# Attention and a phase mixer on one core: shared DMA time in the plan, V by halves, casts on VectorE, fewer fillers

## The chip, the cores and the metric

The kernel runs on one core of a Trainium2 chip. The metric is the time that the device needs for one execution, in microseconds (us). The unprofiled times of one kernel scatter by up to some per cent, and each comes with the mean clock that TensorE (called PE in the profile) was granted. A run is called slow when it is over 1.5% above the fastest of the same kernel.

## The reference

Four batches of 768 positions, eight heads of 64. Heads 0, 2 and 6 attend to everything before them; heads 1, 3, 4, 5 and 7 only to four sink positions and a window of 64. The attention's result goes, head beside head, into a mixer:

```python
scores = np.where(mask, scale * q @ k.T, -1e9)          # mask: causal, or causal & (sink | window)
a = np.exp(scores - max); a = a / (a.sum(-1) + 1e-9)
x = (a @ v)                                             # heads side by side: 768 x 512 per batch
theta = x @ w_theta
zr, zi = x * np.cos(theta), x * np.sin(theta)
u = x + w_tok_r @ zr + w_tok_i @ zi                     # 768 x 768 mixing over positions
out = u + np.maximum(u @ w_ch, 0.0)
```

## The kernel before

The program is a list of more than 800 steps. Each step names the engines that can do it with an estimated duration, what it comes after, and which buffer it takes and gives back. A planner simulates the engines and, whenever one is free, gives it the ready step of highest rank. The resulting order is what the chip runs, engine by engine, and every engine runs its own list strictly in order. The rank is the length of the chain behind a step plus a correction from `TILT`, a list of numbers that an earlier search had found for exactly these durations. Transfers are steps too: "DMA" stands for the queue that GpSimd fills, "DMAH" for the one that SyncE fills.

```python
class Plan:
    COLD = 6000
    SHARE = {}                                   # empty: the branch below never runs
    ...
    def order(self, free):
        ...
                ns = s.on[e]
                if e == "PE" and t < self.COLD:
                    ns *= 1.9
                if e in self.SHARE:              # what the other kind of queue has to do slows this one
                    o = "DMA" if e == "DMAH" else "DMAH"
                    rest = max(0, free.get(o, 0) - t) + sum(...)
                    ns += min(rest, ns * self.SHARE[e]) * (1 - 1 / self.SHARE[e])
```

V of batches 1 to 3 arrives as float32 in one load, is cast to bf16 in four steps of one head pair each (pairs 0+2, 4+6, 1+3, 5+7), and for the five windowed heads a copy `vx` shifted by 64 rows is then made by DMA (the "V move").

```python
        issue = add("SP", 1000, lambda b=b: load_v(b), free_room)
        land = add("DMAH", 8500, None, [issue])
        for n in range(4):
            cast[b, n] = add({"DVE": 480, "POOL": 800}, 0, lambda b=b, n=n: cast_v(b, n), [land] + old, port=True)
        move = add("SP", 1400, lambda b=b: move_v(b), [cast[b, n] for n in (1, 2, 3)] + old)
        moved = add("DMAH", 700, None, [move])
```

Each 128 rows of x go through a transposing DMA into `xT`, for which the plan allowed `add("DMAH", 500, ...)`. Last, where the plan leaves PE idle in the first 30 us, small products without use ("fillers") keep its clock up:

```python
                gap = s.start - busy
                for _ in range(int(gap / 56 * (1 if s.start < 6000 else 0.55))):
                    nc.tensor.matmul(state["idle"][:, :128], ident, ident, start=True, stop=True, skip_group_check=True)
```

The softmax here doesn't subtract the row's maximum and nothing guards it: scores larger than these inputs give would overflow.

Of the kernel before, what the change touches and what calls it, by code (L numbers as in the profile page):

```python
# [25 lines left out]
    -1302, 9909, -1288, -485, 13881, -764, -420, 9549, 13866, 13674, -766, 9551, -9999629, -11630, 0, -913,  # L26
    -11392, 0, -838, 16670, 0, 18999, 0, 31553, -118, 18390, 640, 18361, 17120, 323, 17600, -382, 481, -706, 443,
    -106, 9627, 814, 9657, 561, 2712, 11002, 1146, 772, 492, 1364, 10980, 2378, 11128, 1607, 13772, 5395, 13972,
    5537, 14415, 116734, 16250, 190868, 16177, 80777, 16221, 81513, 392888, 392964, 393917, 393918, 393999, -9479,
    13017, 1168, 12237, 1256, 392649, 10167, 15325, 358, 154648, 429569, -944, 317644, 109627, 1628, 121764, 304,  # L30
    6684, 1805, -213, 0, -243, 0, 48, 0, 268, 2243, 82, 2385, -458, 8, 474, 3988, 15, -215, -298, 0, 1141, 0,
    1856, 0, 1833, 0, 2261, 0, 150, -110, 34, 1686, 2273, 0, 156, -506, -27, -122, -1317, 0, 29087, -609, 0, 4040,
    1057, 1017, 11085, 892, 1518, 554, 1866, -646, 10484, 973, -161, 1791, 1115, -348, 614, 9710, 273623, 9763,
    273460, 14943, 268995, 1069, 1272, 1670, -621, 917, -1392, 1300, 983, 828, 1721, 1204, 788, 13914, 116160,
    13800, 116248, 319905, 111468, 410534, 92438, 428932, 109116, 206113, 142, 317187, 5760, 95832, 2897, 206133,
    7063, 206110, 1716, 206004, -201, 578, 725, 95792, -153, 4546, 243, 95843, 4630, 12925, 22009, 3179, 4454,
    3981, 4172, 4669, 3945, 12929, 301, 3855, 860, 4395, 8714, 2367, 321, 336, 968, 531, 1019, 706, 1009, 206458,
    2077, 206456, 473, 45, 812, 62, 8, -736, 51, 1089, 27, 1778, 891, -55, 1165, -48, 893, -175, -527, 1, 930,
    488, 1010, -62, -733, 382, -249, 0, -685, 717, 1710, -588, 901, 678, 114, 765, 1226, -416, 2106, 938, 1642,
    -315, 1648, 377, -426, 8555, 6819, 2225, 611, 25, 2373, 610, 2258, 523, 709, 1335, 1069, 937, 1050, -298, 532,  # L40
    698, -479, 1572, 983, -715, 2138, 1252, -496, 2446, 4894, -495, 8639, -356, -672, 0, 1234, 5787, -413, 0, 410,
    1675, 1271, 414, 48, 388, 1109, 0, 1477, 626, 1756, 0, 1663, -672, 1819, 0, 1293, 1448, 465, 475, 1243, 1837,
    1295, 162, 1889, 467, 1488, 4474, -383, 1510, -898, 1679, 1682, 1256, 573, 1163, 106, 991, 1250, 445, 1896,
    1055, -143, 2305, 0, 1729, 0, 1172, -41, 1235, 673, -1178, 70, 0, 62, 1728, 885, -356, 621, -59, 12, -872,
    366, -367, 160, -781, -729, 0, 1888, 1965, 931, 1361, 796, 350, 0, 461, -397, 1765, 147, -912, -1367, 0, 947,
    370, 406, 0, 32, 2165, 1039, 535, -222, 4588, 7, 1380, -1639, 0, 91, 161, -49, 1198, -4, -922, 1691, 649, 704,
    0, 598, 1002, 656, 1201, 287, 259, 1980, 537, 695, 0, 162, -2, 160, 398, 403, 869, 183, -829, 396, 278, -834,
    230, 5365, -163, 208, -483, 1861, -530, -483, -2386, 61, -372, -292, -419, -428, -1803, 2, 102, 83, 2198, 431,
    -499, 196, 3468, 868, 259, 772, -1907, 445, -604, 103, 476, -183, 1596, -419, -629, 473, -1976, 9, 2203, 1423,
    984, -133, -560, -699, 147, -398, 97, 532, -1951, -128, 2407, -470, -605, 985, 34, 30, 208, -902, 353, 1767,  # L50
    961, 503, 0, 926, 644, 286, 0, 971, 686, -365, 168, 2865, 887, -284, 3557, 2492, 781, -517, 13, 2255, 1030,
    581, 0, 1052, 2526, 4485, 16764, 1082, 3775, 824, 1247, 11161, 15066, 16794, 18329, 1257, 1430, 1589, 1445,
    3273, 962, 3878, 3597, -465, 3254, -275, 1070, 789, 1102, 1172, 495, 253, 2635, 1324, -549, -338, 100, -173,
    46, 916, 0, 566, 177, -474, 961, 476, -674, 0, 192, 166, 0, -257, 1298, 1455, 0, 536, 273, -666, 568, 0, -951,
    0, -115, -237, 0, 885, 1254, 1597, 0, 226, -184, 1211, 1032, 0, 353, 8, 536, 25, 5, 606, 1260, 940, 0, -318,
    -1004, -993, -1256, 524, 1632, 2091, 553, 306, 0, 1218, 3158, 3117, 646, -614, 2310, 2208, -678, 60, 0, -178,
    3288, 1765, -435, 1010, -528, -134, 2674, 1241, -142, 1700, 650, 1333, 430, 612, 4107, 608, 1342, -164, 922,
    0, 1402, 1418, -709, 1482, 1386, 226, 7011, 123, 2034, 2021, 237, 643, 2159, 1363, 1292, 6888, 3610, -364,
    1026, 2201, 257, 1596, 2209, 925, -719, -151, 2611, 870, 6865, 104, 2247, 3477, 1105, -118, 756, -437, 2154,
    2252, 1513, 168, 7028, 109, 1623, 929, -291, 164, -139, -42, -664, 2046, -672, -57, 208, 793, 807, -552, 76,  # L60
    1555, 979, -786, 149, 1012, 864, 783, 0, 2261, 681, 1275, 6, 2544, 965, -732, 238, 767, -899, 148, 163, 1194,
    307, 1350, 1346, 1481, 1334, 323, 442, 732, 100, 145, 2068, 427, 1946, 3128, 3466, 2104, 2543, 2274, 2477,
    6630, 6388, 2865, -1355, -823, 1522, 1309, -646, 206, 0, 2095, 1904, 665, 23, -1439, 166, -303, 421, -695, 0,
    2218, 2187, 2190, -354, -462, 781, 877, -163, 58, 0, 1127, 692, 2301, 317, -800, 1688, 727, 1856, 880, 0, 38,
    898, 4483, 3686, 135, 4057, 1486, 1226, -116, 0, 796, 661, -2275, -343, -404, 2023, -2016, 404, 1710, 0, 1321,
    1355, 2252, 1553, -616, 1656, 2292, 819, 1306, 0, -680, 359, 1262, 1443, -321, 108, 1175, 589, 1409, 0, -1239,
    -1201, -978, 424, 138, 902, 1222, 138, 891, 0, 2070, 1612, 1785, 865, 480, 983, 4723, 835, 1272, 590, 2316,
    2562, 3059, 885, 4524, 478, 896, 652, 1003, 340, 845, 3709, 3073, 510, -99, 3191, 518, 961, 1059, 492,
# [3 lines left out]
class Step:  # L72
# [6 lines left out]
    def __init__(self, on, fn, after, take, give, mode, bias, port):  # L79
        self.on, self.fn, self.after = on, fn, [a for a in after if a is not None]  # L80
        self.take, self.give, self.mode, self.bias, self.port = take, list(give), mode, bias, port
        self.eng = next(iter(on)) if len(on) == 1 else None
        self.users = 0
        self.slot = self.start = self.end = self.ns = None


class Plan:
# [12 lines left out]
    SHARE = {}  # L100
# [6 lines left out]
    def add(self, on, ns, fn, after=(), take=None, give=(), mode=None, bias=0, port=False):  # L107
        s = Step(on if isinstance(on, dict) else {on: ns}, fn, after, take, give, mode, bias, port)
        for g in s.give:
            g.users += 1  # L110
        self.steps.append(s)
        return s

    def order(self, free):
# [18 lines left out]
        mode = {}  # L133
# [9 lines left out]
        out = []  # L143
# [7 lines left out]
        while events:  # L151
# [10 lines left out]
            for e in engines:  # L162
# [34 lines left out]
                if e in self.SHARE:  # L197
                    o = "DMA" if e == "DMAH" else "DMAH"
                    rest = max(0, free.get(o, 0) - t) + sum(n.on[o] for n in ready.get(o, ()) if ready_at[n.n].get(o, 0) <= t)
                    ns += min(rest, ns * self.SHARE[e]) * (1 - 1 / self.SHARE[e])  # L200
# [26 lines left out]
def kernel(  # L227
# [127 lines left out]
    def load_v(b):  # L355
        nc.sync.dma_start(out=v_room.rearrange("p h j d -> p (h j) d"), in_=v[b].rearrange("h (j p) d -> p (h j) d", p=128))
# [10 lines left out]
    def move_v(b):  # L367
        for s, h in ((slice(0, 1), slice(4, 5)), (slice(1, 5), slice(1, 8, 2))):
            nc.sync.dma_start(out=vx[:64, s], in_=vt[:64, h])
            nc.sync.dma_start(out=vx[64:, s, 1:], in_=vt[64:, h, :NB - 1])  # L370
# [340 lines left out]
    clear_vs_done = add({"DVE": 700, "POOL": 1900}, 0, clear_vs)  # L711
# [11 lines left out]
    for what in "kq":  # L723
        issue = add("SP", 600, lambda what=what: load_first(what), take="st_v", bias=10 ** 6)
        land = add("DMAH", 640, None, [issue])
# [12 lines left out]
    def cast_load(ns, moved, fn, take=None):  # L738
        issue = add("POOL", ns, fn, casting[-1:], take=take, bias=10 ** 6 if len(casting) < 8 else 0)
        casting.append(issue)  # L740
        return issue, add("DMA", moved, None, [issue])
# [30 lines left out]
    def v_steps(b):  # L772
# [9 lines left out]
        free_room = [cast[b - 1, n] for n in range(4)] + [xk[b - 1, 5]] if b > 1 else picked + room  # L782
        issue = add("SP", 1000, lambda b=b: load_v(b), free_room)
        land = add("DMAH", 8500, None, [issue])
        for n in range(4):
            cast[b, n] = add({"DVE": 480, "POOL": 800}, 0, lambda b=b, n=n: cast_v(b, n), [land] + old, port=True)
# [194 lines left out]
```

## Time and profile before

| | before |
|---|---|
| times of four runs, us | 201.62, 202.88, 200.8, 201.1 |
| profiled run: span, mean PE clock | 201.2 us, 0.983 |
| PE busy | 187.3 us (93%) |
| VectorE busy | 130.8 us (65%) |
| DMA | 28.07 MB in 42,302 packets |
| fillers | 106, of them 58 before the first transposes |

How to read it: PE is the engine that can hardly be shortened, so the 14 us in which it was not busy, and the microseconds in which it was busy at half speed, are what there is to win. The prediction shows the lines and prices three holes in PE's row: A at 60 to 68 us, B at 116 to 123 us and C at 91 to 93 us. The profiled run took 203.02 us and is on record as slow. Its low clock stands directly behind holes A and B.

### The profile page before, as it was taken

What the parts mean: (1) busy time and instruction counts of PE and PEld (TensorE: products, weight loads), DVE (VectorE), ACT (ScalarE), POOL (GpSimd) and SP (SyncE); (2) the same over time, 40 slices, a digit from 0 to 9 for tenths busy, and PEclk for the clock granted to TensorE, in tenths of its full rate; (3) what the DMA queues carried; (4) which work ended last, traced back from release to release, by engine and by line L of the source; (5) the groups of instructions that cost most, each with busy time, mean ns of one, the idle gap of its engine ahead of it and who ended that gap; (6) DMA issues with size and microseconds to landing.
All of it is one profiled execution on the core that took longest, in us unless ns stands there. A gap on an engine that the chain in (4) does not pass through costs nothing.

```text
span 201.2 us, 5192 instructions
## 1 busy us (share of the span) xinstructions
PE 187.3 (93%) x2177; PEld 106.8 (53%) x2177; DVE 130.8 (65%) x246; ACT 105.9 (53%) x130; POOL 61.9 (31%) x136
## 2 busy tenths in 40 slices
PE   7999999899995999996999939999999999999982
PEld 7866687545553884442436714554445564444440
DVE  6655597698783775988725720999535748962451
ACT  4597956798772369794555105696573444400010
POOL 7787879031595020163069000023121100000000
PEclk9999999999999799999999988999999999999999
DMA  5999999999389754953259993598453462324422
GB/s 166 156 176 189 205 207 165 162 236 232 63 136 204 96 81 137 224 156 73 104 73 141 158 187 77 146 220 152 101 154 89 114 91 79 103 80 111 127 104 104
DMA packets 42302, 28.07 MB, mean 139 GB/s; under 512 B 21928, under 2 KB 39208, under 8 KB 42280
## 3 DMA queue, kind: packets, MB, share of 16 engines
q1 hardware_dynamic: 29384, 17.65, 38.1%
q0 software_dynamic: 12896, 10.09, 35.0%
q8 instruction: 17, 0.28, 0.6%
q14 instruction: 5, 0.04, 0.1%
HBM read 25.71 MB, written 6.29 MB: 159 GB/s over the span
## 4 chain that ended last, share of the span: by engine, by line
PE 80%; DMA 8%; DVE 7%; ACT 2%; issue 1%; SPq 0%; POOL 0%; DVEq 0%
PE bank L595 27%; PE pair L572 10%; PE bank L618 10%; PE pair L455 9%; PE pair L546 7%; PE bank L388 7%; DMA xT<-x 5%; PE bank L939 4%; DMA vx<-vt 3%; DVE zr L319 2%; PE bank L342 2%; DVE zi L319 2%; DVE vx L316 1%; PE bank L608 1%; PE bank L639 1%; PE bank L558 1%
## 5 line engine op out<-in xcount | busy, mean ns | idle before, releaser
L595 PE MATMUL bank<-zr,wtokTr 128*128 128x512 bf16 x144 | 38.7, 380 | 1.5 <-DVE zr L319 1.5
L595 PE MATMUL bank<-zi,wtokTi 128*128 128x512 bf16 x144 | 38.8, 382 | 0.0
L323 POOL TENSOR_SCALAR_AFFINE_SELECT P<-P 128x256 bf16<-128x256 bf16 (+1 forms) x48 | 17.4, 383 | 49.0 <-ACT P L477 37.2
L477 ACT ACTIVATE P<-pair 128x1024 bf16<-128x1024 f32 (+2 forms) x24 | 21.4, 917 | 14.5 <-PE pair L455 14.5
L572 PE MATMUL pair<-w_theta_sb,xT 128*128 128x512 bf16 x96 | 24.0, 396 | 3.4 <-DMA xT<-x 3.4
L599 DVE TENSOR_TENSOR u<-x,bank 128x512 bf16<-128x512 bf16 x24 | 16.3, 684 | 14.5 <-PE bank L595 14.4
L618 PE MATMUL bank<-w_ch_sb,uT 128*128 128x512 bf16 x96 | 24.5, 380 | 0.7 <-ACT uT L316 0.7
L455 PE MATMUL pair<-qT,kT 64*64 64x128 bf16 (+6 forms) x380 | 24.4, 239 | 0.0
L319 DVE TENSOR_TENSOR zr<-x,ct 128x512 bf16<-128x512 bf16 x24 | 17.1, 745 | 9.8 <-ACT ct L577 9.8
L595 PEld LDWEIGHTS <-wtokTi 128*128 128x128 bf16 x144 | 13.4, 98 | 16.1 <-issue 0.7
L595 PEld LDWEIGHTS <-wtokTr 128*128 128x128 bf16 x144 | 12.9, 98 | 16.6 <-issue 3.2
L622 DVE SCALAR_TENSOR_TENSOR ot<-bank,u 128x512 f32<-128x512 f32 x24 | 16.5, 689 | 5.8 <-PE bank L618 5.4
L577 ACT ACTIVATE ct<-pair,half_pi 128x1024 f32<-128x1024 f32 x12 | 13.3, 1114 | 12.6 <-PE pair L572 10.3
L455 PEld LDWEIGHTS <-kT 64*64 64x64 bf16 (+1 forms) x380 | 12.2, 102 | 14.0 <-issue 10.1
L546 PE MATMUL pair<-vx,P_st 128*128 128x65 bf16 x120 | 15.3, 195 | 2.0 <-DMA vx<-vt 2.0
L553 DVE TENSOR_TENSOR x<-pair,r 128x512 bf16<-128x512 f32 x24 | 16.6, 692 | 0.8
L572 PEld LDWEIGHTS <-xT 128*128 128x128 bf16 x96 | 9.3, 101 | 14.7 <-DMA xT<-x 3.5
L377 POOL COPY kS<-kT 64x4 bf16<-64x4 bf16 x20 | 4.9, 247 | 39.4 <-DVE kT L316 27.7
L319 DVE TENSOR_TENSOR zi<-x,st 128x512 bf16<-128x512 bf16 x24 | 16.9, 735 | 0.0
L474 ACT ACTIVATE P_st<-pair 128x512 bf16<-128x512 f32 (+1 forms) x16 | 12.6, 810 | 6.0 <-PE pair L455 5.9
L546 PE MATMUL pair<-vt,P_st 128*128 128x65 bf16 x120 | 15.4, 195 | 0.0
L546 PE MATMUL pair<-vt,P 128*128 128x65 bf16 x252 | 14.3, 195 | 0.0
(90 smaller groups left out, 296.0 us busy)
## 6 DMA issues: line engine op xcount, KB each, us to landing
out_dram<-ot SPq DMA_DIRECT2D x24, 256.0 KB, 2.2
qb<-in_q_dram POOLq DMA_DIRECT2D x13, 192.0 KB, 6.2
kb<-in_k_dram POOLq DMA_DIRECT2D x13, 192.0 KB, 6.6
wtok<-in_moe_w_tok_r_dram POOLq DMA_DIRECT2D x3, 384.0 KB, 8.6
v_room<-in_v_dram POOLq DMA_DIRECT2D x2, 384.0 KB, 7.8
wtok<-in_moe_w_tok_i_dram POOLq DMA_DIRECT2D x2, 384.0 KB, 8.8
vx<-vt SPq DMA_DIRECT2D x3, 195.0 KB, 7.0
w_theta_sb<-in_moe_w_theta_dram POOLq DMA_DIRECT2D x1, 512.0 KB, 8.3
```

What stands on the lines that cost most here:

```text
L319: {"DVE": nc.vector, "POOL": nc.gpsimd}[state["step"].eng].tensor_tensor(o, a, b, ALU.mult)
L323: nc.gpsimd.affine_select(out=t, in_=t, compare_op=ALU.is_ge, fill=fill, base=base, pattern=pattern, channel_multiplier=cm)
L388: nc.tensor.transpose(pt[64 * x:64 * x + 64, j * 128:(j + 1) * 128], state[what, b][:, h, j * D:(j + 1) * D], ident)
L455: nc.tensor.matmul(ps[half, yy, c:c + w], l, r, start=True, stop=hide is None, skip_group_check=True)
L477: nc.scalar.activation(P.rearrange("p (y c) -> p y c", y=2), ps[:, :, :w0], AF.Exp, scale=scale)
L546: nc.tensor.matmul(o, l, r, start=(m == 0), stop=True, skip_group_check=True)
L553: nc.vector.tensor_tensor(dst, av[:, :, :, :D], r.unsqueeze(3).to_broadcast([128, 2, 4, D]), ALU.mult)
L572: nc.tensor.matmul(ps[:, y], state["xT", b][:, kk, (i + y) * 128:(i + y + 1) * 128], w_theta_sb[:, kk], start=(kk == 0), stop=(kk == KD - 1))
L595: nc.tensor.matmul(py, wtokT[n][:, s, t * 128:(t + 1) * 128], z[:, s], start=(g == 0 and m == 0), stop=(g == 2 and m == 3))
L599: nc.vector.tensor_tensor(u, state["x", b][:, t], state.pop(("py", b, t)), ALU.add)
L618: nc.tensor.matmul(pc, uT[:, kk], w_ch_sb[:, kk], start=(kk == 0), stop=(kk == KD - 1))
L622: nc.vector.scalar_tensor_tensor(ot, state.pop(("pc", b, t)), 0.0, state.pop(("u", b, t)), ALU.max, ALU.add)
```

## The change

The intent: the plan should know that the two kinds of DMA queue slow each other, V should come in two halves so that casting and moving start earlier, GpSimd should no longer cast V, and fillers in the cold first microseconds should be counted at the time that they really take. All of `TILT` was searched anew, so the order of every batch is another. The core of the diff, without `TILT`:

```diff
-    SHARE = {}
...
-                if e in self.SHARE:
+                if s.share:
                     o = "DMA" if e == "DMAH" else "DMAH"
                     rest = ...
-                    ns += min(rest, ns * self.SHARE[e]) * (1 - 1 / self.SHARE[e])
+                    ns += min(rest, ns * s.share) * (1 - 1 / s.share)
...
-        free_room = [cast[b - 1, n] for n in range(4)] + [xk[b - 1, 5]] if b > 1 else picked + room
-        issue = add("SP", 1000, lambda b=b: load_v(b), free_room)
-        land = add("DMAH", 8500, None, [issue])
-        for n in range(4):
-            cast[b, n] = add({"DVE": 480, "POOL": 800}, 0, lambda b=b, n=n: cast_v(b, n), [land] + old, port=True)
-        move = add("SP", 1400, lambda b=b: move_v(b), [cast[b, n] for n in (1, 2, 3)] + old)
-        moved = add("DMAH", 700, None, [move])
+        for half in range(2):
+            issue = add("SP", 920, lambda b=b, half=half: load_v(b, half), [cast[b - 1, n] for n in (half, half + 2)] if b > 1 else picked + room)
+            land = add("DMAH", 4100, None, [issue], share=2)
+            for n in (half, half + 2):
+                cast[b, n] = add("DVE", 480, lambda b=b, n=n: cast_v(b, n), [land] + old, port=True)
+        moved = []
+        for s, h, pairs in ((slice(0, 1), slice(4, 5), [1]), (slice(1, 5), slice(1, 8, 2), [2, 3])):
+            move = add("SP", 1220, lambda s=s, h=h: move_v(s, h), [cast[b, n] for n in pairs] + old)
+            moved.append(add("DMAH", 500 if h.stop == 5 else 900, None, [move], share=4))
...
-                xk[b, i] = add("DMAH", 500, None, [issue])
+                xk[b, i] = add("DMAH", 600, None, [issue], share=5)
...
-            landed[what, b, n] = add("DMA", 1100, None, [issue])
+            landed[what, b, n] = add("DMA", 1080, None, [issue], share=1.5)
...
-                for _ in range(int(gap / 56 * (1 if s.start < 6000 else 0.55))):
+                for _ in range(int(gap / 56 * (0.5 if s.start < 5500 else 0.55))):
```

Cut besides: the transposes of u get `share=5`, the stores `share=2`, q is loaded before k at the start, and two start-up durations differ.

## The prediction

> **What bounds the kernel now.** I read the page's 40 slices first, then the waits of TensorE (PE), then five-microsecond windows around the thin slices, then the timeline of the first ten microseconds. The slices (rows: PE, VectorE, granted PE clock, DMA) say that PE is the engine to count on: nine tenths or more in nearly all, and two of its three holes stand beside full DMA slices and are followed by a lower clock.
>
> ```profile
> PE   7999999899995999996999939999999999999982
> ...
> DVE  6655597698783775988725720999535748962451
> ...
> PEclk9999999999999799999999988999999999999999
> DMA  5999999999389754953259993598453462324422
> ```
>
> Between 30 and 125 us PE sat idle behind three things that matter (columns: total us, times, longest):
>
> ```profile
> PE pair L572 <- DMA xT<-x: 3.4, 1, 3.4
> PE pair L546 <- DMA vx<-vt: 2.0, 1, 2.0
> PE bank L595 <- DVE zr L319: 1.5, 1, 1.5
> ```
>
> The windows price them (PE, weight load, VectorE, ScalarE, GpSimd busy; clock; DMA share; GB/s). The reader is to see the idle time and then the clock after it.
>
> ```profile
> 60.00:65.00 5.00, 2.96 (x27) 1.55 (x28) 1.72 (x4) 1.41 (x3) 2.98 (x6) 0.95 1.19 209
> 65.00:70.00 5.00, 5.00 (x105) 4.27 (x103) 3.84 (x9) 1.82 (x2) 0.36 (x2) 0.71 0.80 108
> ...
> 90.00:95.00 5.00, 3.33 (x26) 1.38 (x22) 4.79 (x7) 2.06 (x3) 2.12 (x2) 1.00 0.31 74
> ...
> 115.00:120.00 5.00, 1.63 (x37) 1.30 (x35) 2.06 (x4) 0.00 (x0) 0.00 (x0) 0.91 1.30 173
> 120.00:125.00 5.00, 5.00 (x18) 1.97 (x17) 0.00 (x0) 1.87 (x2) 0.00 (x0) 0.75 0.58 115
> ```
>
> Hole A, 60 to 68 us: PE idles 2.04 us behind the shifted copy of V; one-microsecond windows then show clocks of 0.74, 0.50, 0.50 and 0.55 from 64 to 68 us, which costs 0.26+0.50+0.50+0.45 = 1.7 us. Together 3.75 us. Hole B, 116 to 123 us: 3.37 us idle behind the transposed copy of x for the third batch, then 0.16 us of work at 0.55 and three windows at 0.50, 0.50 and 0.74, 1.3 us. Together 4.7 us. Hole C, 91 to 93 us: 1.50 us behind a VectorE product, with neighbours 1.67 us. Under one microsecond more lies at 25 to 40 us. The middle therefore loses about 11 us of 201. From 125 to 195 us PE is full at clock 1.00: nothing to win there except fewer mode switches.
>
> Hole B is a DMA queue problem: from 100 to 122 us GpSimd issued eight q and k loads, and the transposes issued by SyncE took 8.5 us to land against 3.0 us in the median of the whole run.
>
> ```profile
> kb<-in_k_dram POOLq DMA_DIRECT2D x4, 192.0 KB, 5.9
> qb<-in_q_dram POOLq DMA_DIRECT2D x4, 192.0 KB, 5.8
> ...
> xT<-x SPq DMA_TRANSPOSE x6, 8.5
> ```
>
> Hole C is a casting problem. GpSimd did all four casts of V here (1.16 us each), and the VectorE products beside them took 1.27 us each, where their pairs elsewhere take 0.64 (1.28 for two at 39.05 us).
>
> ```profile
> 87.49 4.63 POOL L316 CAST vt<-v_room 128x768 bf16<-128x768 f32 x4 [5.10 <-DMA v_room<-in_v_dram]
> ```
> ```profile
> 87.66 2.54 DVE L319 TENSOR_TENSOR zi<-x,st 128x512 bf16<-128x512 bf16 x2
> 90.13 2.53 DVE L319 TENSOR_TENSOR zr<-x,ct 128x512 bf16<-128x512 bf16 x2
> ```
>
> The start: 58 small filler products hold PE to 7.2 us, although q was cast by 4.76 us and k by 6.67 us.
>
> ```profile
> 1.43 5.79 PE L939 MATMUL bank<-ident 128*128 128x128 bf16 x58 [1.43 <-POOL ident L648]
> ...
> 3.93 0.83 ACT L316 CAST qb<-v_room 128x768 bf16<-128x768 f32 x1 [1.83 <-DMA v_room<-in_q_dram]
> ...
> 5.84 0.83 ACT L316 CAST kb<-v_room 128x768 bf16<-128x768 f32 x1 [1.08 <-DMA v_room<-in_k_dram]
> ...
> 7.16 0.53 PE L388 MATMUL bank<-ident,qb 128*64 128x128 bf16 x12
> ...
> 7.77 0.53 PE L388 MATMUL bank<-ident,kb 128*64 128x128 bf16 x12
> ```
>
> **What the Trainium skill says.** "TensorE: Matmul & The Clock Gate", section "Wait — 56ns, not 53.3ns?", gives 106.7 ns between 128-column products on a cold array and 55.6 ns warm. The trace agrees: 5.79 us / 58 = 100 ns for the first fillers, and the code counted them at 56. The same page, section "What's actually happening", says the clock halves after an idle window of about 3.4 us; here 2.04 us of idle was enough to be followed by 0.50, so I price a hole at its idle plus about half of it again or more. "DMA: Bandwidth & Descriptors", section "Queues, rings and completion order", says that each DMA engine takes turns between the queues that have work, packet by packet; that fits 8.5 against 3.0 us. "SBUF — State Buffer", section "Who interferes with whom", says that a VectorE instruction with two SBUF inputs contends with a GpSimd one that reads SBUF; the products at 1.27 against 0.64 us agree.
>
> **The change part by part.** No tensor product is added or removed but fillers, so the floor of PE work stays.
>
> 1. Sharing in the plan. The order of all instructions comes from a list plan. Before, it gave an x transpose 0.5 us of transfer plus 2 us of latency, alone or not; now 0.6 us times up to 5 when the other kind of queue has work, so 0.6+2.4 = 3.0 us plus 2. That is near the quiet 3.0 us and nearer the crowded 8.5, though still short by 3.5. The V move was 0.7+2 = 2.7 us and took 7.0; it is now up to 0.9+2.7 = 3.6 plus 2, or 5.6. So the new priorities were found against holes A and B and should put other PE work (the 62 us of mixing products are the stock: 288 x 216 ns) in front of both. The plan was 7.0-2.7 = 4.3 us wrong at A and will be about 1.4 wrong; at B 6.0 wrong and will be 3.5. If the leftover error is what PE sees, A shrinks by 2.9/4.3 = two thirds and B by 2.5/6.0 = four tenths: 3.75 x 0.67 + 4.7 x 0.42 = 4.5 us.
>
> 2. V by halves. The batch's V load becomes two of four heads, each freed by its own casts, and the V move two steps, the first after one cast. In the second batch the load took 14.1 us (issued 38.4, landed 52.5) and PE stood at 61.7 for a move issued at 56.6. With halves, two casts and the move of one head lie under the second half's load; behind the last landing remain two casts of 0.56 us instead of four. That is about 1 us earlier for the last move. It belongs to A and I count 0.3 us more of it. In the third and fourth batch V is off PE's path.
>
> 3. Casts on VectorE alone. Five GpSimd casts become 5 x 0.56 = 2.8 us of VectorE, busy 65%. At C four of them cost 4 x 0.56 = 2.2 us and give back the 4 x 0.63 = 2.5 us by which four products were slow: even in VectorE time. But the list may now place the casts before or after the products that PE waits for, so I take half of C: 0.8 us.
>
> 4. Fillers. The gap was planned at about 58 x 56 = 3.25 us; at half, 29 fillers x 100 ns = 2.9 us end at 4.3 us. q's transposes can start at 5.0 instead of 7.16 us, and k's at about 6.9 instead of 7.77. The later of the two feeds the scores: 0.9 us earlier. But DMA shares are above 1 from 5 to 35 us, and 49 more fillers after 7.2 us show PE waiting there for loads, which fillers cannot bring. I count 0.4 us. Turning q before k in the text changes little: the trace has q first already (issued 0.82, k 1.34).
>
> Sum: 4.5+0.3+0.8+0.4 = 6.0 us. Against it stands the price of a new order: every batch is rearranged, and a plan that is wrong by microseconds makes a new hole somewhere. I charge 1.2 us, about one hole as small as C. Net 4.8 us: 201.6-4.8 = 196.8 us, a ratio of 0.976.
>
> **The rivals.** (a) The holes move rather than shrink: the same eight loads of the fourth batch have to be carried at some time, about 190 GB/s is all that DMA moved when full, and the next waiting transposes or V moves meet them instead. For it: the first 60 us are full of DMA. Against it: from 125 us on DMA shares are mostly 0.3 to 0.6, so there is room. It would give 200 to 202 us. (b) VectorE becomes the bound: 2.8 us more casts come in one burst of 2.3 us per batch, and the u and x steps behind them hold PE. For it: VectorE is at nine or ten tenths at 40 to 45 and 90 to 95 us. Against it: the casts on GpSimd had slowed it by as much. It would give 199 to 201 us. (c) Nearly all of the 11 us come back, because the priorities were searched anew: 190 to 192 us with the start. For it: PE is full for the last 70 us under the old order already. Against it: crowded transfers are still under-counted. (d) The early V loads, which no longer wait for the previous batch's last transpose of x, run beside those transposes and stretch them; that would cost one to two microseconds at B's place.
>
> **Range and chances.** The middle of (a) and (b) is about 200.5, of (c) 191. I put 0.1 on (c), 0.3 on (a), (b) or (d) in strength, and the rest around 196.5. A step of 2% is 4.0 us, so below 197.6 us. My sum passes it by 0.8 us only. Prediction 196.8 us, range 192.3 to 201.0; faster 0.58, same 0.37, slower 0.05.
>
> **What would show it.** Step 1 is right if PE's waits behind the x transpose and the V move fall from 3.4 and 2.0 us to about 2 and 0.7, and the windows after them keep a clock near 1.00; it is wrong if either stays with another name or place. Step 2: two V loads per batch, and the last V move issued within 2 us of the second's landing. Step 3: no V cast on GpSimd, and VectorE products at 0.6 to 0.7 us throughout the stretch of the casts; mean of the z products down from 0.74 us. Step 4: about 29 fillers before the first transposes, which start near 5 us; the first normalisation of x (27.4 us before) shows what of it survives. The prediction fails if PE's idle time between 25 and 195 us does not fall below 6 us (about 8 now), or if the start slips because fewer fillers leave the clock cold for the first transposes.

## The result

| | before | changed |
|---|---|---|
| median of the runs taken together, us | 201.36 (200.8 to 202.88) | 195.15 (192.77 to 199.09) |
| profiled run: span, clock | 201.2, 0.983 (slow) | 191.0, 1.00 (fast) |
| PE busy | 187.3 us (93%) | 180.7 us (95%) |
| VectorE busy | 130.8 us | 127.9 us |
| packets for 28.07 MB | 42,302 | 56,174 |
| fillers | 106 (58 first) | 80 (29 first) |

The ratio of the fast runs is 0.957 (0.948 to 0.966). Ratios here are the mean time of one kernel's fast runs over that of the other's fast runs of the same rounds, so not quite the ratio of the medians in the table. The changed kernel has two clear states: 193.11 and 192.77 us at clocks of 1.00 and 0.995, 199.09 and 197.19 us at 0.965 and 0.972. Compared at full clock alone, the two runs of the kernel before that had it in all rounds took 198.96 and 199.56 us, those of the changed one 193.1 to 193.4 us: about 6 us.

The slices of the changed kernel's profiled (fast) run, the rows PE, VectorE, clock, DMA as in the prediction:

```profile
PE   6979999999999899999999999999999999999982
...
DVE  7655397789975568899547534999734657953551
...
PEclk9999999999999999999999999999999999999999
DMA  5999999999599995499999959313314554215232
```

The three thin places of PE are gone and so is the low clock. The DMA row says where the transfers went: it is full over most of the slices from 48 to 110 us, which had gaps before. The waits of PE between 30 and 125 us, the list that before began with 3.4, 2.0 and 1.5 us, now begins:

```profile
PE bank L611 <- DVE u L602: 0.5, 1, 0.5
PE pair L575 <- issue: 0.3, 2, 0.2
```

The windows of the old holes (PE, weight load, VectorE, ScalarE, GpSimd busy; clock; DMA share; GB/s):

```profile
60.00:65.00 5.00, 5.00 (x64) 2.85 (x62) 0.64 (x2) 3.59 (x6) 1.78 (x3) 1.00 1.03 202
...
90.00:95.00 5.00, 5.00 (x36) 1.86 (x38) 3.26 (x6) 3.93 (x5) 2.46 (x6) 1.00 1.18 220
115.00:120.00 5.00, 4.79 (x96) 3.60 (x95) 2.84 (x6) 1.95 (x3) 0.00 (x0) 1.00 1.21 139
120.00:125.00 5.00, 5.00 (x54) 2.65 (x54) 5.00 (x10) 4.24 (x5) 0.00 (x0) 1.00 0.35 100
```

In each, PE is full (the 4.79 is partly a few matmul records that the trace lacks) at clock 1.00, beside DMA shares of 1.0 to 1.2 in three of the four. The places of A and B are nearly as crowded as before (1.19 at 60 us, 1.30 at 115 us); what is different is that PE has something else to do. This is PE's line in the kernel before on which hole A ends:

```profile
63.72 0.19 PE L546 MATMUL pair<-vx,P_st 128*128 128x65 bf16 x1 [2.04 <-DMA vx<-vt]
```

PE had begun this group of products, the values of the second batch, at 61.37 us, came to those that need the larger part of the V move at 61.7 us, and idled 2.04 us in their midst. In the changed kernel the same group starts at 63.46 us and runs through: the new order has put about two microseconds of other work in front, as much as the hole was long. The moves themselves were issued no earlier (55.8 to 57.9 us, before 55.3 to 57.9). For the third batch, the transposes of x were issued from 103.2 us instead of 109.7, and six of the eight loads of the fourth batch had gone by 102 us.

VectorE's products and the casts of V, from the page and from its timeline:

```profile
L321 DVE TENSOR_TENSOR zr<-x,ct 128x512 bf16<-128x512 bf16 x24 | 15.7, 682 | 1.3 <-ACT ct L580 1.3
```
```profile
49.01 1.03 DVE L318 CAST vt<-v_room 128x768 bf16<-128x768 f32 x2
...
53.40 1.21 DVE L318 CAST vt<-v_room 128x768 bf16<-128x768 f32 x2
```

The mean product fell from 745 to 682 ns, and the first cast of the second batch came at 49.01 us instead of 52.55. Now the bookkeeping: the span fell by 201.2 - 191.0 = 10.2 us. The holes held 2.04 + 3.37 + 1.67 = 7.1 us of idle time and 3.0 us of clock, 10.1 us together. That the two agree so closely is partly chance: the first normalisation of x comes at 27.73 us, before at 27.15, so the start gave nothing in this run and cost 0.6 us, and the new wait behind u costs 0.5 us. Some 1.2 us of the 10.2 therefore have no name. The start's timeline on PE:

```profile
1.44 3.27 PE L944 MATMUL bank<-ident 128*128 128x128 bf16 x29 [1.44 <-POOL ident L651]
4.94 0.85 PE L391 MATMUL bank<-ident,qb 128*64 128x128 bf16 x12 [0.23 <-ACT qb L318]
...
11.19 0.53 PE L391 MATMUL bank<-ident,qb 128*64 128x128 bf16 x12 [0.64 <-DMA qb<-in_q_dram]
...
14.56 0.86 PE L391 MATMUL bank<-ident,kb 128*64 128x128 bf16 x24 [0.93 <-DMA kb<-in_k_dram]
```

29 fillers instead of 58, and q's transposes at 4.94 instead of 7.16 us, but twelve of them still take 0.85 us instead of 0.53, and PE then arrives early at two loads and idles 0.64 and 0.93 us. That detail becomes important below.

### The profile page after: what moved, and what is told of

It reads as the page before. It is cut to its first block, busy times and chain, and to the rows that moved or that the text cites. A ratio compares the mean times of both kernels' runs of the same rounds, so it can differ in the third digit from the quotient of the medians.

```text
span 191.0 us, 5124 instructions
## 1 busy us (share of the span) xinstructions
PE 180.7 (95%) x2126; PEld 103.1 (54%) x2151; DVE 127.9 (67%) x247; ACT 104.9 (55%) x130; POOL 59.2 (31%) x133
## 2 busy tenths in 40 slices
DMA packets 56174, 28.07 MB, mean 147 GB/s; under 512 B 40408, under 2 KB 53080, under 8 KB 56152
## 4 chain that ended last, share of the span: by engine, by line
PE 81%; DMA 11%; POOL 2%; issue 2%; DVE 1%; ACT 0%; POOLq 0%; DVEq 0%
PE bank L598 30%; PE pair L575 11%; PE bank L621 10%; PE pair L549 9%; PE pair L458 8%; PE bank L391 6%; DMA vx<-vt 5%; DMA kb<-in_k_dram 4%; PE bank L344 2%; DMA vs_f<-in_v_dram 2%; PE bank L642 1%; PE bank L944 1%; PE bank L561 1%; PE bank L611 1%; PE pair L525 1%
## 5 line engine op out<-in xcount | busy, mean ns | idle before, releaser
L598 PE MATMUL bank<-zr,wtokTr 128*128 128x512 bf16 x140 | 37.9, 380 | 0.4 <-issue 0.2
L598 PE MATMUL bank<-zi,wtokTi 128*128 128x512 bf16 x136 | 36.7, 379 | 0.5 <-issue 0.3
L621 PE MATMUL bank<-w_ch_sb,uT 128*128 128x512 bf16 x90 | 24.0, 380 | 1.2 <-ACT uT L318 0.7
L458 PE MATMUL pair<-qT,kT 64*64 64x128 bf16 (+6 forms) x380 | 23.7, 238 | 0.0
L575 PE MATMUL pair<-w_theta_sb,xT 128*128 128x512 bf16 x89 | 22.2, 379 | 0.7 <-issue 0.5
L380 POOL COPY kS<-kT 64x4 bf16<-64x4 bf16 x20 | 7.1, 355 | 49.1 <-ACT kT L318 43.5
L598 PEld LDWEIGHTS <-wtokTi 128*128 128x128 bf16 x144 | 13.6, 98 | 15.6
L458 PEld LDWEIGHTS <-kT 64*64 64x64 bf16 (+1 forms) x380 | 12.4, 102 | 14.8 <-issue 10.2
L580 ACT ACTIVATE ct<-pair,half_pi 128x1024 f32<-128x1024 f32 x12 | 13.4, 1117 | 10.2 <-PE pair L575 6.7
L321 DVE TENSOR_TENSOR zr<-x,ct 128x512 bf16<-128x512 bf16 x24 | 15.7, 682 | 1.3 <-ACT ct L580 1.3
L321 DVE TENSOR_TENSOR zi<-x,st 128x512 bf16<-128x512 bf16 x24 | 15.6, 683 | 0.1
L477 ACT ACTIVATE P_st<-pair 128x1024 bf16<-128x1024 f32 (+1 forms) x16 | 12.8, 810 | 3.4 <-PE pair L458 2.7
L621 PEld LDWEIGHTS <-uT 128*128 128x128 bf16 x96 | 8.6, 98 | 10.2 <-ACT uT L318 0.8
```

Of the source, the lines that this page charges most:

```text
L321: {"DVE": nc.vector, "POOL": nc.gpsimd}[state["step"].eng].tensor_tensor(o, a, b, ALU.mult)
L458: nc.tensor.matmul(ps[half, yy, c:c + w], l, r, start=True, stop=hide is None, skip_group_check=True)
L575: nc.tensor.matmul(ps[:, y], state["xT", b][:, kk, (i + y) * 128:(i + y + 1) * 128], w_theta_sb[:, kk], start=(kk == 0), stop=(kk == KD - 1))
L580: nc.scalar.activation(t, state["th", b, i], AF.Sin, bias=half_pi)
L598: nc.tensor.matmul(py, wtokT[n][:, s, t * 128:(t + 1) * 128], z[:, s], start=(g == 0 and m == 0), stop=(g == 2 and m == 3))
L621: nc.tensor.matmul(pc, uT[:, kk], w_ch_sb[:, kk], start=(kk == 0), stop=(kk == KD - 1))
```

## The experiments

Twelve kernels ran, in three groups of four, each group on one chip beside the kernel before (medians 201.79, 201.58 and 201.75 us, so the chips agree). The theory was three separate holes, each with a cause of its own, plus the clock that a hole costs afterwards; and the whole gain of the change as the sum of them. The main rivals: the new order as a whole is what pays, or the holes only move. So I took the old kernel with its old order and undid one hole at a time (runs b_), and took parts out of the changed kernel (runs a_).

### b_castdve: the old order, no cast of V on GpSimd

```diff
     order = plan.order(...)
+    for b in range(1, B):
+        for n in range(4):
+            cast[b, n].eng = "DVE"
```

> The kernel before, its order kept, with all twelve casts of V set to VectorE. Theory (the three holes are the 10.2 us): the VectorE products near 88 us take 0.64 us instead of 1.27, PE's wait of 1.5 us at 91 to 93 us goes, and the time falls by 1 to 2 us. Rival (the gain is the new order as a whole, the holes only show where slack sits): within 0.5 us of before, the idle time reappears in the next 20 us.

Measured: median 200.99 us, ratio 0.990 (0.978 to 1.002), unclear. Hole C was gone: PE was busy for all of 90 to 95 us at clock 1.00, and the two z products behind it took 1.29 us, 0.64 each. But a new hole stood in the second batch. PE's waits and VectorE's timeline:

```profile
PE bank L595 <- DVE uT L316: 1.7, 1, 1.7
```
```profile
52.33 0.56 DVE L316 CAST vt<-v_room 128x768 bf16<-128x768 f32 x1 [2.47 <-DMA vs_f<-in_v_dram]
```

VectorE runs its list in order, and the cast that had been GpSimd's now stood in that list before its data had come. VectorE idled 2.47 us and the copy of uT behind the cast kept PE waiting 1.7 us. PE also waited 1.1 us for a load of q, and hole A's wait was absent: the V move landed at 61.8 us, and PE came to the first product that needs it only at 62.6 us. So the contention was real (1.27 against 0.64 us a product), but what its removal is worth in time this run does not show. Casting on VectorE is only good where the data is there by then.

### b_late: the old order, six of the eight crowding loads held back

```diff
+    late = [the GpSimd loads of q and k of batch 3, except k0 and q1]
+    gate = add("POOL", 100, lambda: nc.gpsimd.tensor_copy(half_one, state["xT", 2][:1, 0, 3 * 128:3 * 128 + 1]))
+    ...                      # gate and loads placed right after the transpose of block 3 of batch 2
```

(Batches are counted from 0 in code.) The gate is a copy of one element of the transposed x, so that the loads can start only when block 3 of six has landed.

> The kernel before with six of the fourth batch's eight q and k loads held back until the third batch's fourth transposed block of x has landed (a one-element copy on GpSimd waits for it). Theory: the transposes then land in about 3 us instead of 8.5, the wait of 3.4 us near 118 us and the half clock after it go, and the time falls by 3.5 to 5 us. Rival (the loads have to run at some time): the fourth batch's q and k then come late near 130 us and the time changes by less than 1 us.

Measured: median 203.91 us, ratio 1.001 (0.993 to 1.009). This was a miss in the design. The one transpose of the six whose landing the profile gives took 4.1 us instead of 8.5 (that, too, is one of six), but the last of them was issued just when the gate had let the loads go. The chain of waits and PE's wait in this run:

```profile
117.83 7.50 DMA xT<-x
```
```profile
PE pair L573 <- DMA xT<-x: 2.5, 1, 2.5
```

The crowd met the last block instead: 7.50 us. It shows that the loads do stretch the transposes and that later is not the direction to move them. It does not show what hole B is worth.

### b_warm: the old order, 34 fillers in front of hole A

```diff
         pav = mine()
+        if (b, i) == (1, 0):
+            for _ in range(34):
+                nc.tensor.matmul(pav[:, 0, :128], ident, ident, start=True, stop=True, skip_group_check=True)
```

The hole stays and only the clock behind it should be saved.

> The kernel before with 34 small filler products put ahead of the second batch's first values, so that PE has work in most of the 2.04 us hole near 62 us. Theory (the half clock from 64 to 68 us is caused by the hole and costs 1.7 us): the clock stays at 1.00 there and the time falls by 1 to 1.7 us. Rival (the clock fell for another reason): the same 0.5 clock appears, the time stays within 0.5 us or grows.

Measured: median 200.42 us, ratio 0.995 (0.988 to 1.003); three runs at 200.25 to 200.42 and one at 204.26. In the profile PE was full at clock 1.00 from 60 to 70 us, where the kernel before had 0.95 and 0.71. That fits a half clock caused by A's idle time, but it does not show it. This whole profile has a mean clock of 1.00; the kernel before reached that in two runs without these fillers (198.96 and 199.56 us, faster than this one), and b_warm's other three runs were at 0.985, 0.975 and 0.985. Hole B, too, passed without a lower clock here (2.9 us of waiting in two pieces, span 198.4 us), which already says that the price of a hole is not the same from run to run.

### b_halves: the old order, V as two loads, head 4 moved as soon as it is cast

```diff
     def load_v(b):
-        nc.sync.dma_start(out=v_room..., in_=v[b]...)
+        for half in range(2):
+            heads = slice(4 * half, 4 * half + 4)
+            nc.sync.dma_start(out=v_room[:, heads]..., in_=v[b, heads]...)
...
+    for b in range(1, B):
+        first = add("SP", 0, lambda b=b: move_v(b, ((slice(0, 1), slice(4, 5)),)))
+        ...                                  # placed right after the cast of heads 4 and 6
```

> The kernel before, its order kept, with each V load as two DMAs of four heads and the move of head 4 issued right after its cast. Theory (V by halves is a small part of hole A): the last move lands at most 1 us earlier and the time falls by 0 to 1 us. Rival (the halves are what removed hole A): the wait of 2.0 us behind the V move goes and the time falls by 3 to 4 us.

Measured: median 202.67 us, ratio 0.999 (0.986 to 1.011). By the time alone, nothing. At a like clock, 0.991, its one run of 199.6 us stands against 201.89 and 201.44 us of the kernel before on the same chip. The windows of its profile (a slow run at 0.962):

```profile
60.00:65.00 5.00, 5.00 (x112) 3.83 (x109) 3.91 (x10) 2.17 (x4) 0.51 (x3) 1.00 1.31 176
...
85.00:90.00 5.00, 3.33 (x19) 1.13 (x17) 5.00 (x7) 2.45 (x3) 2.51 (x3) 0.97 0.27 59
90.00:95.00 5.00, 5.00 (x27) 2.43 (x27) 1.62 (x4) 1.96 (x4) 0.29 (x1) 0.50 0.11 32
```

Hole A is gone entirely: the first cast began at 49.74 us instead of 52.55 (about 1.1 us of this only because the load was issued at 37.2 instead of 38.35 us), the moves were issued from 53.65 instead of 55.33 and the longest took 3.2 us instead of 7.0. But hole C, 1.67 us of idleness as before, was now followed by clock 0.50 over about seven microseconds of full PE, and the half clock behind hole B lasted 6.8 us instead of 3.4. One hole's gain was paid out as clock behind the others. A time alone would have called the halves worthless; the windows of this one profile say that they remove hole A.

### b_early: the old order, all eight loads of the last batch right after the third batch's V casts

```diff
+    loads = {landed[what, 3, n].after[0] for what in "qk" for n in range(4)}
+    early = [s for s in order if s in loads]
+    order = [s for s in order if s not in loads]
+    at = order.index(cast[2, 3]) + 1
+    order[at:at] = early
```

> The kernel before with all eight q and k loads of the fourth batch issued about 12 us earlier, right after the third batch's V casts near 92 us, so that they are gone when the x transposes start. Theory (these loads crowd the transposes and make hole B): the transposes land in about 3 us, no transposed block is waited for over 1 us near 118 us, the time falls by 3 to 5 us. Rival (the loads only meet something else): a new wait of the same size between 90 and 110 us, time within 1 us.

Measured: 196.74 us (195.6 to 197.68, all fast, clock 0.998 to 1.0), ratio 0.979 (0.972 to 0.987). The window of the old hole:

```profile
115.00:120.00 5.00, 5.00 (x49) 2.70 (x46) 1.49 (x3) 2.29 (x2) 0.00 (x0) 1.00 0.42 82
```

PE full, clock 1.00, and DMA share 0.42 instead of 1.30. The transpose whose landing the profile gives took 2.4 us instead of 8.5, with `TILT` and all other orders untouched. That settles what made hole B: it was the crowd. Fast runs against fast runs, moving eight issues wins 4.1 us (on record as unclear, because the interval reaches over the 2% line). Part of it is clock: at a clock of 1.00 the kernel before took 198.96 and 199.56 us, b_early 197.1 us in the mean of three runs. Smaller waits stand elsewhere, 1.3 us behind a transposed u and 0.8 us behind a load of q. The loads now went from 90.2 to 95.9 us instead of 101.8 to 110.7, into a stretch in which DMA had stood idle for two thirds of the time (share 0.31 at 90 to 95 us before).

### b_three: the three remedies together in the old order

The halves of b_halves, the early loads of b_early, and the casts of the third batch alone on VectorE (`cast[2, n].eng = "DVE"`). The old fillers and the old priorities stay.

> The kernel before, its order kept but for three edits at once: V by halves with head 4 moved first, the third batch's V casts on VectorE, and the fourth batch's loads early. Theory (the gain of the change is these three holes and the half clocks after them): 193 to 196 us, within 2 us of the changed kernel's fast runs. Rival (the searched order as a whole is needed): 198 us or more, new holes take the place of the old.

Measured: 192.62 us (five fast runs at 191.84 to 192.79, one slow at 196.29), ratio 0.958 (0.952 to 0.964). Its slices:

```profile
PE   6999999999999999999999999999999999999982
...
PEclk9999999999999999999999999999999999999998
```

No thin slice between the second and the last two, and waits of PE of at most 0.7 us from 30 us on. The three remedies together give the whole gain of the change, and about one microsecond more, without the new order. So they suffice; that the changed kernel gains by closing the same holes is read from its own windows above. This is the best kernel.

### after_again: the changed kernel, six more runs

No edit.

> The changed kernel once more, for its states. Four runs so far: 193.1 and 192.8 at clock 1.00, 199.1 and 197.2 at 0.965 and 0.972. Theory (the slow runs are the clock falling to a half after some idle stretch of PE, by chance of its phase): again two clusters, 192 to 194 at a clock over 0.99 and 196 to 200 at 0.96 to 0.98. Rival (chip to chip noise): one cluster.

Measured: fast 193.37, 193.43 and 194.43 us; slow 198.61, 198.96 and 199.33 us at clock 0.964 to 0.965; ratio of the fast runs 0.965 (0.957 to 0.973). With the first four, five of ten runs of the changed kernel were slow. This time the profile fell into such a run, and the windows of its start show what the state is:

```profile
10.00:12.00 2.00, 0.22 (x4) 0.04 (x1) 0.14 (x1) 0.95 (x1) 2.00 (x5) 1.00 1.07 132
12.00:14.00 2.00, 1.57 (x17) 0.93 (x19) 0.61 (x1) 0.00 (x0) 0.35 (x1) 0.58 1.35 186
14.00:20.00 6.00, 6.00 (x67) 3.97 (x67) 3.53 (x5) 2.96 (x4) 2.67 (x7) 0.50 1.45 197
```

At 10 to 12 us PE had 0.22 us of work: it had come 2.2 us too early to the second load of q, whose transposes started at 12.43 us (in the fast profile the wait was 0.64 us and they started at 11.19). Then the clock was 0.50 until about 26 us, although PE was always busy. So in this profile the slow state is made in the first twelve microseconds, by a load that PE meets sometimes closely and sometimes 2 us too early.

### a_fillmore, a_fill: the changed kernel with more fillers

```diff
-                for _ in range(int(gap / 56 * (0.5 if s.start < 5500 else 0.55))):
+                for _ in range(int(gap / 56 * (0.5 if s.start < 5500 else 1.0))):    # a_fillmore
+                for _ in range(int(gap / 56 * (1 if s.start < 6000 else 0.55))):     # a_fill: the old count
```

> The changed kernel with the later fillers (5.5 to 30 us) doubled, from 0.55 to 1.0 of the planned gap. Theory (PE's idle 1.6 us between 10 and 15 us is what lets the clock fall in the slow runs): no run below clock 0.98, all runs at 192 to 195. Rival (the clock falls elsewhere, or fillers delay real work): slow runs remain, or all runs are 1 us or more longer.

> The changed kernel with the fillers counted as before (58 instead of 29 ahead of the first transposes). Theory (the filler count is worth at most 0.4 to 0.9 us in the middle and the early clock is safer with more of them): fast runs 0 to 1 us longer than the changed kernel's. Rival (the start is a large part of the gain): 2 us or more longer.

Measured for a_fillmore: 198.5 us, ratio 0.985 (0.977 to 0.993), unclear by the 2% line. No run below 0.985 in clock, but every run late. Fillers in every gap may delay the real work, but the profile (a slow run of 200.57 us) shows other things too: k's first cast came at 7.62 us instead of 5.44, PE waited 2.05 us for it, and the clock was 0.50 from 9 to 12 us. What made every run late is open.

Measured for a_fill: 195.15 us (194.44 to 195.82 and one of 197.91), no run at a clock below 0.991. Its profile has 58 fillers in 5.54 us, q's transposes from 6.90 us, and waits of only 0.2 and 0.6 us at the two loads. In the median of the fast runs it is 195.13 - 193.43 = 1.7 us slower than the changed kernel. The start does not hold this loss: the first normalisation of x came at 27.85 us, in the changed kernel at 27.73. It stands at 30 to 37 us, in two pauses of PE of 0.5 and 1.1 us, in which PE waited for nothing that the profile shows; the changed kernel has none there. In return the state at 0.965 did not appear, and the mean of its six runs is 195.5 us, that of after_again's six 196.4 us.

### a_stop: the changed kernel with 35 fillers just in front of the two loads

```diff
+            for n, steps in ((20, [kept["q", 0, 3], kept["q", 0, 2]]), (15, [kept["k", 0, 2], kept["k", 0, 3]])):
+                if s is min((x.after[0] for x in steps), key=lambda x: x.start):
+                    for _ in range(n):
+                        nc.tensor.matmul(state["idle"][:, :128], ident, ident, start=True, stop=True, skip_group_check=True)
```

> The changed kernel with 20 fillers ahead of the transposes that wait for the second q load near 11 us and 15 ahead of those that wait for the second k load near 14 us. Theory (the slow runs start in that starved stretch): clock at or over 0.98 in nearly all runs, 193 to 195.5 us, median below the changed kernel's 196. Rival (the stretch stays too empty, or fillers delay real work): slow runs at 0.965 stay, or the fast ones are 1 us or more longer.

Measured: 196.22 us, all six runs between 194.61 and 196.35 at clock 0.994 to 1.00; ratio 0.975 (0.969 to 0.981), unclear by the 2% line. The slow state is gone, which supports that it comes from the wait for the second loads. But the fast state is gone too: the median is about 2.8 us above 193.4. The 35 products themselves are not what costs: the first normalisation came at 27.90 us, 0.17 us later than in the changed kernel. As in a_fill, the loss stands at 30 to 38 us, in two pauses of PE:

```profile
PE pair L549 <- issue: 1.2, 1, 1.2
PE bank L561 <- issue: 1.1, 1, 1.1
```

"Issue" is time in which PE waited for nothing that the profile shows, so the cause of these pauses is open. With the changed kernel's fillers (the changed kernel itself, after_again, a_whole, a_castpool) 11 of 18 runs had a clock of 0.972 or less, with more fillers (a_fillmore, a_fill, a_stop) none of 18. That it is the wait for the second load of q that starts the slow state rests on two slow profiles, with waits of 2.2 and 2.0 us, against one fast one with 0.64. So a_stop supports the cause and is no remedy.

### a_whole: the changed kernel and its order, V as one load again

```diff
+    for b in range(1, B):
+        for kind, n, whole in (("load", (0, 1), lambda b=b: load_whole(b)), ("move", (False, True), move_both)):
+            one, two_ = sorted((pieces[kind, b, x] for x in n), key=lambda s: s.start)
+            one.fn, two_.fn = None, whole        # the earlier half does nothing, the later one all of it
```

> The changed kernel, its order kept, with each V load as one DMA at the later half's place and both moves at the later move's place. Theory (with the new order V by halves matters little): within 1 us of the changed kernel. Rival (the halves carry hole A): PE waits again 2 us or more behind the V load or move near 64 us, and the time is 3 to 5 us longer.

Measured: 201.25 us; only one fast run, 197.1 at 0.991, so no ratio. That run is 197.1 - 193.4 = 3.7 us above the changed kernel's. PE's new wait and what VectorE waited for:

```profile
PE bank L620 <- DVE u L611: 2.7, 1, 2.7
```
```profile
52.63 1.13 DVE L318 CAST vt<-v_room 128x768 bf16<-128x768 f32 x2 [3.48 <-DMA v_room<-in_v_dram]
```

The casts that ran at 49.01 us have their data at 52.63, VectorE idles 3.48 us and everything behind it in its list is late. The same form of damage as in b_castdve. The order was planned for halves, so this says that the new order rests on them, not what halves would give to an order planned without. PE had no wait behind the V move here, though both moves now left at the later one's place. But the 2.7 us and a half clock behind them (0.50 from 56 to 58 us) held PE up, and it came to the products that need the move only at 68.3 us, against 63.5. Whether the new order would keep hole A shut without the halves is therefore not shown.

### a_castpool: the changed kernel, third batch's four casts on GpSimd

```diff
+    for n in range(4):
+        cast[2, n].eng = "POOL"
```

> The changed kernel with the third batch's four V casts given back to GpSimd, their places kept. Theory (the casts on VectorE alone matter as far as VectorE products lie beside them): products beside the casts double to about 1.2 us, up to 2 us longer if PE waits for them. Rival (no part of the gain): within 0.5 us of the changed kernel at the same clock.

Measured: 197.77 us; one fast run at 194.15, three at clocks of 0.965 to 0.972, and the profile again shows the start of after_again (2.0 us of waiting for q, then half clock). That one fast run is within 0.8 us of the changed kernel. In GpSimd's timeline:

```profile
78.49 3.14 POOL L318 CAST vt<-v_room 128x768 bf16<-128x768 f32 x4 [9.41 <-DMA out_dram<-ot]
```

0.79 us a cast, where in hole C it was 1.16. While they ran VectorE did normalisations and u sums, which took 0.69 and 0.68 us as always, and the z products came only from 84.70 us on, at 0.64. So it was not the engine of the casts alone that made hole C, but that they lay beside the z products, which took 1.27 us there.

### What could not be run

Two kernels would have separated the plan's sharing term from the new priorities: the changed one without sharing, and the old one with it. For both the planner found no order at all, because the priorities were searched for the one set of durations only. They were never built, and what the sharing term did for the search stays open.

## Why the prediction was right or wrong

The time was right: 195.15 us against 196.8, inside the range. That it came so near is partly luck: no run took about 195 us, the median is the middle between two states at 193 and at 197 to 199 us, and the prediction had foreseen one state. The mechanism was right too: the gain is three holes and the clock behind two of them, and PE's waits from 25 us to its last product fell from about 8 to 2.4 us, where the prediction had set 6 as the limit. The size of several terms was off, in both directions.

**Step 1, holes A and B.** "If the leftover error is what PE sees, A shrinks by 2.9/4.3 = two thirds and B by 2.5/6.0 = four tenths", leaving waits of 2 and 0.7 us. Both are zero, so this was the term mis-sized most: 4.5 us predicted, while A and B held 3.75 + 4.7 = 8.45 us and the profile has all of it back. The reasoning took the plan's error for PE's wait. But a plan need not know a transfer's duration, only put enough work in front or carry the load where nothing waits: about two microseconds more of other work stand before the V move's products, as much as the hole. One number under the sum was thin: 8.5 us is the landing of a single transpose, the only one of the six that the profile gives. For B, the old order with eight issues moved lost no time at 115 to 120 us either (b_early). Whether the sharing term led the search there or the search would have found it without is open, as said.

**Step 2, halves, "0.3 us".** Too small in what it can do, and the sign named for it failed. In its one profile b_halves has neither the idle time of hole A nor the half clock behind it (3.75 us in the kernel before), though its times are no shorter, and a_whole lost 3.7 us in its only fast run. Yet in the changed kernel the last V move of the second batch was issued at 57.25 us, more than two microseconds after the casts of the second half had ended (54.6 us): the first move had stood 5.3 us at the head of SyncE's list. The halves earn their keep there by letting VectorE cast at 49 us without waiting, not by an earlier move. Steps 1 and 2 cannot be told apart as terms of a sum: the changed kernel closed hole A with moves issued no earlier than before, b_halves with earlier ones in the old order, and a_whole does not decide, because PE came to the place late.

**Step 3, casts, 0.8 of 1.67 us.** Hole C came back in full. The contention was seen rightly (1.27 against 0.64 us; b_castdve removes it). The worry that the list "may now place the casts before or after the products that PE waits for" was also right, in b_castdve: a cast placed too early cost 1.7 us. The new order avoided it. a_castpool adds, by one fast run, that with the new placement GpSimd could have kept the casts at a cost of under a microsecond.

**Step 4, fillers, 0.4 us.** The counts came exactly: 29 fillers, transposes at 4.94 us ("near 5 us"). Of the 0.4 us nothing is seen where the prediction wanted to look for it: the first normalisation of x came at 27.73 us, against 27.15 before and 27.85 in a_fill, which has the old count in the same order. a_fill's fast runs are 1.7 us slower all the same, by the pauses at 30 to 37 us, whose cause is open. And the failure that the prediction's last sentence names, fewer fillers leaving a cold clock, came partly true and one step later: PE now runs into the second loads, waits up to 2.2 us, and half of the runs pay about 5 us for it. In six runs each the old count was 0.9 us better in the mean.

**The price of a new order, 1.2 us.** Small in the profile: 0.5 us behind u, and the two waits at the start. b_three, which pays no such price, has fast runs at 191.8 to 192.8 us against 192.8 to 194.4, one microsecond in the mean; some of that is the start, where its first normalisation stood at 26.22 us in the profile.

**The rivals.** (a), the holes move, failed for the change but describes b_late and, in part, b_castdve; its "about 190 GB/s is all that DMA moved when full" is a mean, and slices of 232 and 236 GB/s stand on the page. (b), VectorE as the bound, failed: 67% busy, no long wait behind it. (c), "nearly all of the 11 us come back", was nearest in the fast state, at 192.8 to 194.4 us, about one to four microseconds above its 190 to 192. I had given it 0.1. The median is at 195 only because half of the runs lose it again at the start. (d), V loads that stretch the transposes, left no wait.

**Clock.** "A hole at its idle plus about half of it again or more" was about right on average in that one profile (3.0 us of clock for 7.1 us of idle time) and wrong as a rule. Hole C cost nothing behind it in the kernel before and 3.4 us in b_halves. What the traces show instead is a step. Add up the shortfall, 2 x (1 - clock) for each one-microsecond window, and PE's clock was halved for 3.4 us at A and at B, for 3.4 us once each in b_castdve, b_late, a_whole and a_fillmore, for 6.8 us twice in b_halves, and for 13.7 and 13.6 us at the start of after_again and a_castpool: each about a whole multiple of 3.4. So by this estimate a hole is followed by nothing or by a loss of up to 1.7, 3.4 or 6.8 us; what decides between these is open. At full clock on both sides, the gain should be the idle time alone: 7.1 us, less the 0.5 us behind u and the 0.6 us of a later start, makes 6.0, and the full-clock runs differ by about 6.

## What to carry to other kernels

When several holes stand in one engine's row, judge a remedy by the windows of its own hole, since the time of a single remedy can be swallowed by the clock behind the next one, and then run the remedies together. Before rearranging everything, try moving the few transfers that crowd a latency-critical one into the stretch where the DMA row is thin: eight moved issues alone gave a ratio of 0.979 (0.972 to 0.987), against 0.957 and 0.965 for the new order of the whole program. And work that is moved to an in-order engine brings its wait along: it belongs where its data has already landed, or everything behind it waits too.

## What the Trainium skill lacked or had wrong

- "TensorE: Matmul & The Clock Gate", section "What's actually happening", gives about 3.4 us for the idle window that halves the clock and about the same of busy time to get it back, with a free-running window. Here shorter idle stretches were followed by 0.50: 2.04 us before hole A's half clock, 1.67 us in b_halves, 2.2 us in after_again; and the same 1.67 us was followed by nothing in the kernel before, which a free-running window would allow. The way back fits the page's 3.4 us behind A and B (3.4 us each), but it took twice as long in b_halves (6.8 us behind hole C, with PE full) and four times in after_again (13.7 us, with many small products and transposes); why it takes one, two or four times is open. The 106.7 ns for a cold 128-column product in section "Wait — 56ns, not 53.3ns?" fits the end of a range: 58 fillers took 81 ns each in b_three, 96 in a_fill, 100 before and 108 in b_warm, as the clock came up earlier or later.
- "DMA: Bandwidth & Descriptors", section "Queues, rings and completion order", describes the turn-taking between queues but gives no size for a transposing transfer beside crowding loads. Here it was 8.5 us beside eight loads of 192 KB and 2.4 us with the loads moved away (b_early), each the one landing of six that the profile gives, and the issuing of such a transpose on SyncE also stretched, from 1.21 us in the median of b_early to 1.57 us.
- None of the pages gives a figure for splitting a load by heads: 42,302 packets became 56,174 for the same 28.07 MB, and the casts could nevertheless begin earlier in b_halves (49.74 instead of 52.55 us, of which about 1.1 us is that the load was issued earlier).
